# Weight conversion in a fused attention and two-expert kernel: background work placed by running sums of engine time, fetches on GpSimd's queue, all first-product weights through scratch

## The chip, the cores and the metric

The kernel runs on one core of a Trainium2 chip. TensorE (PE) multiplies, VectorE (DVE) and ScalarE (ACT) compute on tiles, GpSimd (POOL) and SyncE (SP) issue DMA transfers here. The metric is the time of one execution on the device in microseconds (us); less is better.

## The reference

What is computed, cut to its core (4 batches, 12 heads, 448 positions, head size 64; DM = 768, DFF = 2048; 1792 tokens):

```
scores = np.matmul(q, k.transpose(0, 1, 3, 2)) / np.sqrt(64) - np.log(448)
x = np.matmul(1.0 / (1.0 + np.exp(-scores)), v)      # to (1792, 768)
h = x @ moe_w_in                                     # (768, 2048)
x = (h - np.tanh(h)) @ moe_w_out                     # (2048, 768)
h = x @ moe2_w_in
out = (np.maximum(h, 0) + alpha * np.minimum(h, 0)) @ moe2_w_out
```

The activations are float32, and the four weight matrices are float64.

## The kernel before, in words

**Numbers.** Every product runs in float16 with two halves per operand: a value is scaled, its high half is its rounding to float16, and its low half is what is left (x*s - high). Three matmuls per tile pair (high-high, high-low, low-high) are added up in PSUM. A "split" writes both halves of a tile: ACT the high one, DVE the low one.

**Stages.** TensorE goes through 5088 matmul instructions in this order. Attention: 12 groups `g` of two head pairs, each with scores (L353, sigmoid on ACT in L355) in seven parts `u`, and values (L371, L377; float32) that add into one PSUM tile `ps3`, which DVE copies out (L384) and searches for its maximum (L300). The first product (`product(0, ...)`, L398): 16 column blocks `f` by 2 token halves `sb`, 36 matmuls each, with a chain of ACT and DVE operations after each (L655 to L664) that ends in a COPY_PREDICATED (L663). The second product (`product(1, ...)`, L398): 6 column blocks `e` by two halves, 96 matmuls each; its operands are the results `g` of the first, split by `split_job` (L292, L293) once their scale is known (`scale_jobs`, L247 to L262). Then the second expert by Strassen's scheme: seven products by four quarters `q` by two halves, 18 matmuls each, into (L744) and out (L826). Its operands are split in L425 and L426; PSUM results are copied in L751 and added in L756.

**Weights.** A float64 weight comes in as pairs of int32 words, in 64 "units" of six 128x128 blocks (768 KB). `load_unit` fetches one into one of two buffers `stage0`, `stage1` (L104, on SP's queue). Three DVE operations (L110, L112, L114) turn the pairs into float32 words; a split follows (L128, L129 for the first two matrices, L154, L155 for the quarters of the second expert's matrices, where sums and differences of four units are made first, L165 to L183). The 16 units of the first matrix stay in slots; all others are written to scratch in DRAM by GpSimd's queue (L134, L156) and read again by SP's when needed (L219 for the second matrix, L558 for the quarters). There are 53 general slots of 128x896 float32; a slot that is released is given to the next that asks.

**Order.** The conversion is a generator (`conv`), and `bg(us)` takes steps from it, or from the waiting `jobs`, until their estimated lengths reach the number given. These numbers are written at each place of the program: `1.2*len(us)` after each part of attention, 2.2 or 4.0 in the first product, 17.0 in the second, 0.4 to 3.0 in the second expert. `ahead` bounds how many units attention may convert. The order in which an engine runs its instructions is then fixed by a scheduler when the program is built, and each engine and each queue goes through its own list in that order.

Of the kernel before, what the change touches and what calls it, by code (L numbers as in the profile page):

```python
# [35 lines left out]
NG = NP // 2  # L36
# [20 lines left out]

@with_exitstack
def body(ctx: ExitStack, tc, qkd, vd, w1, w2, w3, w4, al, out):
    nc = tc.nc  # L60
    V, A, PE = nc.vector, nc.scalar, nc.tensor
# [7 lines left out]
    scratch.update({(1, u): dr_pool.tile([128, 2 * UN * 128], F16, name=f"scr1_{u}") for u in range(NU)})  # L69
# [30 lines left out]
    def load_unit():  # L100
        i = loaded[0]
        if i < 4 * NU:
            src = wd[i // NU][i % NU].bitcast(I32)
            nc.sync.dma_start(out=stage[i % NSTAGE].rearrange("p a b -> p (a b)"), in_=src)  # L104
            loaded[0] += 1

    def words(i, w):
# [3 lines left out]
        yield 0.57  # L111
        V.scalar_tensor_tensor(w, hi, -0x40000000, w, ALU.bitwise_and, ALU.bitwise_or)  # L112
        yield 0.96
        V.scalar_tensor_tensor(w, lo, 29, w, ALU.logical_shift_right, ALU.bitwise_or)  # L114
        load_unit()
        yield 0.96

    def pair_of(s):
        return s.bitcast(F16)[:, 0:2 * UN * 128].rearrange("p (a c) -> p a c", a=2)

    def conv():
        for i in range(2 * NU):
            w = w32[i % 2]
            yield from words(i, w)
            wf = w.bitcast(F32)
            s = alloc()
            v = pair_of(s)
            A.activation(v[:, 0], wf, AF.Copy, scale=SW)  # L128
            V.scalar_tensor_tensor(v[:, 1], wf, SW, v[:, 0], ALU.mult, ALU.subtract)  # L129
            nconv[0] += 1  # L130
            if i < NU:
                wslot[0, i] = s
            else:
                nc.gpsimd.dma_start(out=scratch[1, i - NU], in_=s.bitcast(F16)[:, 0:2 * UN * 128])  # L134
                release(s)
            yield 0.96
        for m in (2, 3):
            for q in range(NQ):
                yield from quarter(m, q)


    def quarter(m, q):
# [8 lines left out]
        def put(pr, s, scale=SW2):  # L151
            t = alloc()
            v = pair_of(t)
            A.activation(v[:, 0], fl(s), AF.Copy, scale=scale)  # L154
            V.scalar_tensor_tensor(v[:, 1], fl(s), scale, v[:, 0], ALU.mult, ALU.subtract)  # L155
            nc.gpsimd.dma_start(out=scratch[m, pr, q], in_=t.bitcast(F16)[:, 0:2 * UN * 128])  # L156
            release(t)
            return 0.96
# [7 lines left out]
        yield 0.87  # L166
        yield put(5, r)
        yield put(4, a22, -SW2)
# [4 lines left out]
        yield 0.87  # L173
        yield put(6, r)
        V.tensor_tensor(fl(a21), fl(a11), fl(a21), ALU.subtract)
        yield 0.87
        yield put(7, a21)
        release(a21)
        yield put(1, a11)
# [4 lines left out]
        yield 0.87  # L184
        yield put(3, r)
        release(r)
        yield put(2, a12)
# [8 lines left out]
    ahead = [4 * NU]  # L196

    def conv_step(force=False):
        if nconv[0] >= 4 * NU or (not force and (len(free) <= reserve[0] or nconv[0] >= ahead[0])):
            return None  # L200
        return next(conv_gen, 0.0)

    def weight(m, n):
        while (m, n // UN) not in wslot:
            if m:
                load_second(n // UN + 1)
            else:
                conv_step(True)
# [3 lines left out]
    second = [0]  # L212

    def load_second(upto):
        while second[0] < min(upto, NU):
            while nconv[0] <= NU + second[0]:
                conv_step(True)
            t = alloc()
            nc.sync.dma_start(out=t.bitcast(F16)[:, 0:2 * UN * 128], in_=scratch[1, second[0]])  # L219
            wslot[1, second[0]] = t  # L220
            second[0] += 1
# [65 lines left out]
    def split_job(d, key, g):  # L287
        def f():
# [3 lines left out]
            A.activation(v[:, 0], src, AF.Copy, scale=s_of(g))  # L292
            V.scalar_tensor_tensor(v[:, 1], src, s_of(g), v[:, 0], ALU.mult, ALU.subtract)  # L293
# [29 lines left out]
    def split_pair(i, parts=1):  # L323
# [4 lines left out]
        for j in range(parts):  # L328
            sl = slice(j * n, (j + 1) * n)
            if parts > 1 and j:  # L330
                V.tensor_scalar(v[:, 0, sl], t[:, sl], SQK, None, ALU.mult)  # L331
            else:
                A.activation(v[:, 0, sl], t[:, sl], AF.Copy, scale=SQK)  # L333
        for j in range(parts):
            sl = slice(j * n, (j + 1) * n)
            V.scalar_tensor_tensor(v[:, 1, sl], t[:, sl], SQK, v[:, 0, sl], ALU.mult, ALU.subtract)  # L336
# [25 lines left out]
    def values(g, u):  # L362
# [18 lines left out]
        if u == 6:  # L381
            b, j = divmod(g, H // 4)
# [39 lines left out]
    def split_to(src, n, g):  # L422
        t = alloc()
        v = hl(t)
        A.activation(v[:, 0, 0:n], src[:, 0:n], AF.Copy, scale=s_of(g))  # L425
        V.scalar_tensor_tensor(v[:, 1, 0:n], src[:, 0:n], s_of(g), v[:, 0, 0:n], ALU.mult, ALU.subtract)  # L426
# [109 lines left out]
    def bgo(us, most):  # L536
        while us > 0 and ojobs and len(opo) < most and len(free) > 6:
            us -= ojobs.pop(0)()
# [37 lines left out]
    if True:  # L576
# [15 lines left out]
        last = None  # L592
        for g in range(NG):
# [3 lines left out]
            if g == NG // 2:  # L597
                jobs.extend(scale_jobs(0, KD))
                jobs.extend(unit_jobs(0))
                jobs.extend(split_job(x, (j, b), 0) for b in range(2) for j in range(KD // 2))  # L600
            ahead[0] = 4 * g // 5
            for n, us in enumerate(groups):
# [9 lines left out]
                if last is not None:  # L612
                    for u in last[1]:
                        values(last[0], u)
                        if u == 6 and last[0] + 3 <= NG - 1:
# [290 lines left out]
```

## Time and profile before

| what | us |
|---|---|
| median of 3 timed runs (1024.02 to 1029.5) | 1025.11 |
| the profiled execution, its own time | 1028.73 |
| span of its trace | 1027.0 |
| TensorE busy | 963.3 |
| VectorE busy | 720.9 |
| ScalarE busy | 577.6 |

The profiled execution lies 3.6 us above the median. A trace gives each instruction's start and length on its engine, and for idle time what ended it. The granted clock of TensorE is 1.00 at 2.4 GHz and 0.50 at 1.2 GHz; a window's mean lies between.

### The profile page before, as it was taken

The numbers are of one execution on the slowest core, as the hardware profiler recorded it, in microseconds if no ns is written. First come the engines' busy times: TensorE is split into PE (matmuls) and PEld (weight loads), VectorE is DVE, ScalarE is ACT, GpSimd is POOL, SyncE is SP. The second block draws the span as 40 slices with busy tenths as digits, with TensorE's granted clock in tenths as the row PEclk, the third lists the DMA queues.
The fourth block names the chain that finished last, engine by engine and source line by source line (L and its number), as shares of the span: only waits on it lengthen the run. The fifth ranks groups of instructions, "written<-read, shape, count | busy, mean of one in ns | idle before, by whom it ended". The sixth has DMA issues, their size and how long they took to land. (4 is left out here: it accounts for less than half of the span.)

```text
span 1027.0 us, 13246 instructions
## 1 busy us (share of the span) xinstructions
PE 963.3 (94%) x5280; PEld 468.2 (46%) x5280; DVE 720.9 (70%) x869; ACT 577.6 (56%) x708; POOL 43.9 (4%) x87
## 2 busy tenths in 40 slices
PE   6888999999999998999499986999999999999998
PEld 2222335555555554555254542455555544555554
DVE  5845749988898897899898788844444789664200
ACT  7777867988999898433333226533333636434200
POOL 0000000000000000111111110000000000000000
PEclk9998999999999998999799998899999999999999
DMA  9833311222242401487888763432522336346301
GB/s 357 294 133 115 117 50 44 81 74 93 77 170 77 138 21 43 165 307 284 305 302 302 267 224 119 152 115 87 161 85 77 93 94 210 108 162 211 120 28 54
DMA packets 42398, 151.87 MB, mean 148 GB/s; under 512 B 5344, under 2 KB 8672, under 8 KB 42336
## 3 DMA queue, kind: packets, MB, share of 16 engines
q1 hardware_dynamic: 36576, 122.71, 36.0%
q0 software_dynamic: 5760, 28.32, 7.3%
q8 instruction: 41, 0.67, 0.3%
q14 instruction: 21, 0.17, 0.0%
HBM read 117.19 MB, written 33.82 MB: 147 GB/s over the span
## 5 line engine op out<-in xcount | busy, mean ns | idle before, releaser
L398 PE MATMUL ps<-slot,slot 128*128 128x448 f16 x2304 | 440.6, 355 | 18.5 <-DMA slot<-scr 14.6
L398 PEld LDWEIGHTS <-slot 128*128 128x128 f16 x2304 | 226.2, 98 | 233.2 <-DMA slot<-scr 13.3
L744 PE MATMUL ps<-slot,slot 128*128 128x448 f16 x1008 | 196.2, 358 | 15.8 <-ACT slot L751 9.8
L826 PE MATMUL ps<-slot,slot 128*128 128x448 f16 x1008 | 193.9, 354 | 4.6 <-ACT slot L425 2.6
L744 PEld LDWEIGHTS <-slot 128*128 128x128 f16 x1008 | 99.9, 99 | 111.9 <-issue 22.5
L826 PEld LDWEIGHTS <-slot 128*128 128x128 f16 x1008 | 99.0, 98 | 99.3 <-issue 8.9
L425 ACT ACTIVATE slot<-slot,sc 128x896 f16<-128x896 f32 (+1 forms) x78 | 77.1, 1026 | 76.4 <-PE ps L826 38.2
L154 ACT ACTIVATE slot<-slot 128x768 f16<-128x768 f32 x56 | 46.7, 842 | 114.9 <-DVE slot L114 56.1
L426 DVE SCALAR_TENSOR_TENSOR slot<-slot,sc,slot 128x896 f16<-128x896 f32 (+1 forms) x78 | 85.8, 1134 | 35.5 <-ACT slot L425 35.3
L355 ACT ACTIVATE slot<-ps,cst 128x896 f32<-128x896 f32 x84 | 79.8, 1004 | 21.4 <-PE ps L353 21.4
L371 PE MATMUL ps<-slot,slot 128*64 128x448 f32 x288 | 66.3, 584 | 11.5 <-DVE slot L384 10.9
L353 PE MATMUL ps<-slot 64*128 64x448 f16 (+1 forms) x576 | 59.8, 368 | 8.9 <-DVE slot L331 4.9
L756 DVE TENSOR_TENSOR slot<-ps,slot 128x896 f32<-128x896 f32 x24 | 26.2, 1090 | 50.9 <-ACT slot L751 46.1
L155 DVE SCALAR_TENSOR_TENSOR slot<-slot,slot 128x768 f16<-128x768 f32 x56 | 51.9, 951 | 1.1 <-ACT slot L154 1.0
L661 DVE SCALAR_TENSOR_TENSOR slot<-ps,sc,slot 128x896 f32<-128x896 f32 x32 | 36.7, 1148 | 22.2 <-ACT slot L659 22.2
L293 DVE SCALAR_TENSOR_TENSOR slot<-slot,sc,slot 128x896 f16<-128x896 f32 x44 | 48.1, 1145 | 4.5 <-ACT slot L292 4.5
L751 ACT ACTIVATE slot<-ps 128x896 f32<-128x896 f32 x24 | 21.8, 908 | 48.5 <-PE ps L744 48.5
L353 PEld LDWEIGHTS <-slot 64*128 64x128 f16 (+1 forms) x576 | 22.4, 100 | 56.7 <-issue 38.4
L292 ACT ACTIVATE slot<-slot,sc 128x896 f16<-128x896 f32 x44 | 42.7, 1029 | 7.3 <-DVE sc L261 7.3
L336 DVE SCALAR_TENSOR_TENSOR slot<-slot,slot 128x896 f16<-128x896 f32 (+1 forms) x25 | 26.3, 1051 | 25.6 <-ACT slot L333 25.5
L762 ACT ACTIVATE slot<-slot 128x896 f32<-128x896 f32 x24 | 22.7, 947 | 37.4 <-DVE slot L761 37.4
L664 ACT ACTIVATE slot<-slot,sc 128x896 f32<-128x896 f32 x32 | 33.3, 1039 | 13.2 <-DVE slot L663 13.2
(78 smaller groups left out, 841.4 us busy)
## 6 DMA issues: line engine op xcount, KB each, us to landing
stage<-w SPq DMA_DIRECT2D x64, 768.0 KB, 4.6
slot<-scr SPq DMA_DIRECT2D x128, 384.0 KB, 3.2
scr<-slot POOLq DMA_DIRECT2D x72, 384.0 KB, 3.2
slot<-qk SPq DMA_DIRECT2D x23, 448.0 KB, 7.3
slot<-v SPq DMA_DIRECT2D x12, 448.0 KB, 6.3
out_t<-slot SPq DMA_DIRECT2D x24, 224.0 KB, 2.0
slot<-qk SPq DMA_DIRECT2D x2, 224.0 KB, 2.6
alpha<-al SPq DMA_DIRECT2D x1, 8.0 KB, 7.3
```

The lines of the kernel that those rows point to most:

```text
L154: A.activation(v[:, 0], fl(s), AF.Copy, scale=scale)
L155: V.scalar_tensor_tensor(v[:, 1], fl(s), scale, v[:, 0], ALU.mult, ALU.subtract)
L292: A.activation(v[:, 0], src, AF.Copy, scale=s_of(g))
L293: V.scalar_tensor_tensor(v[:, 1], src, s_of(g), v[:, 0], ALU.mult, ALU.subtract)
L353: PE.matmul(p[rows, h, 0:S], v[r, jk, S + c * 128:S + c * 128 + m], v[r, jq, 0:S], start=(n == 0), stop=(n == 2), skip_group_check=True)
L355: A.activation(two(a), p[:, :, 0:S], AF.Sigmoid, scale=1.0 / (8.0 * SQK * SQK), bias=cst[:, 0:1])
L371: PE.matmul(p[64 * h:64 * h + 64, i, 0:S], v[:, o:o + 64], a[:, h], start=(c == 0), stop=False, skip_group_check=True)
L398: PE.matmul(p[:, b, 0:S], w[:, i], act(k, sb, b)[:, j], start=(k == 0 and (i, j) == (0, 0)), stop=(k == nk - 1 and (i, j) == (1, 0)))
L425: A.activation(v[:, 0, 0:n], src[:, 0:n], AF.Copy, scale=s_of(g))
L426: V.scalar_tensor_tensor(v[:, 1, 0:n], src[:, 0:n], s_of(g), v[:, 0, 0:n], ALU.mult, ALU.subtract)
L744: PE.matmul(p[:, i, 0:S], w[:, x1, 3 * i + c], a[:, x2], start=fresh and c == 0 and n == 0, stop=c == 2 and n == 2, skip_group_check=True)
L826: PE.matmul(bank(banks[e]), w[:, x1, 2 * e + c], a[:, x2, c * S:(c + 1) * S], start=pr in (1, 2, 5) and q == 0 and c == 0 and n == 0, stop ...
```

## The change

There are five parts.

1. A class `Engine` wraps the three compute engines and adds an estimated length of each instruction to a running sum (`V.t`, `A.t`, `PE.t`) as the program is written out. An operation that touches PSUM starts no earlier than the sum of TensorE. `bg(lead, most)` now emits background work while the sum of DVE (or of ACT, less `most`) is behind that of TensorE; the hand-written numbers and `ahead` go. In the trace of the changed kernel all such operations have the line of the wrapper's call (L81).
2. A split puts its high half on DVE if DVE's sum is behind ACT's (`halves_of`), else on ACT as before. In the built program 70 high halves have moved: 46 of 128x896 and 24 of 128x768.
3. The stage fetches go from SP's queue to GpSimd's (L133).
4. The 16 units of the first matrix go through scratch too (L161, L251): 16 more writes (88 in all) and 16 more reads by SP. Two or three units are loaded ahead of their use instead of five at the start of the second product.
5. In attention the values lag two parts behind their scores instead of one, and background work is also placed ahead of the copy of a group.

```diff
+class Engine:
...
+            if op == "matmul":
+                part = args[0].shape[0] * args[0].shape[1] / 16384
+                self.t += part * n * (1.68e-3 if args[0].dtype == F32 else 0.421e-3) + (0.01 if part < 1 else 0.0)
+            else:
+                if any(a.space == bass.MemoryType.PSUM for a in used):
+                    self.t = max(self.t, self.pe.t)
+                    rate = 1.04e-3
+                else:
+                    rate = 0.52e-3 if op == "tensor_scalar" else 1.04e-3
+                self.t += n * (0.83e-3 if op == "activation" else rate) + (0.26 if op == "activation" else 0.16)
+            return f(out, *args, **kw)
...
-            nc.sync.dma_start(out=stage[i % NSTAGE].rearrange("p a b -> p (a b)"), in_=src)
+            nc.gpsimd.dma_start(out=stage[i % NSTAGE].rearrange("p a b -> p (a b)"), in_=src)
...
+    def halves_of(hi, lo, src, scale):
+        if V.t + 0.4 < A.t:
+            V.tensor_scalar(hi, src, scale, None, ALU.mult)
+        else:
+            A.activation(hi, src, AF.Copy, scale=scale)
+        V.scalar_tensor_tensor(lo, src, scale, hi, ALU.mult, ALU.subtract)
...
+    def load_units(upto):
+        while taken[0] < min(upto, 2 * NU):
+            i = taken[0]
+            while nconv[0] <= i:
+                conv_step(True)
+            t = alloc()
+            nc.sync.dma_start(out=t.bitcast(F16)[:, 0:2 * UN * 128], in_=scratch[i])
...
-    def bg(us):
-        while us > 0:
+    def bg(lead=0.0, most=1.0):
+        while max(V.t, A.t - most) < PE.t + lead:
             if jobs:
-                us -= jobs.pop(0)() or 0.0
-                continue
-            c = conv_step()
-            if c is None:
+                jobs.pop(0)()
+            elif not conv_step():
+                V.t = max(V.t, PE.t + lead - 2.0)
                 return
-            us -= c
...
         if u == 6:
+            if g:
+                bg(-1.0, 4.0)
...
-            ahead[0] = 4 * NU
-            if f >= KF - 2:
-                load_second(3 * (f - KF + 2) + 2 * sb)
-            bg(4.0 if (jobs and f > 8) else 2.2)
+            load_units(f + 3 if sb == 0 else 0)
+            bg()
...
-            load_second((min(e + 1, KD) * KF + UN - 1) // UN + 1)
+            load_units(NU + (min(e + 1, KD) * KF + UN - 1) // UN + 1)
             reserve[0] = 3
-            ahead[0] = 4 * NU
...
-            bg(17.0)
+            bg()
```

How the built order moves, in three places. In the rows a name's last number is the program's own; `scr1_2` before and `scr_18` after are the same unit of the second weight, `scr1_9` and `scr_25` another.

SP's queue before, ahead of the second product:

```order
L219 DMA slot14_149<-scr1_1_120 128x1536
L219 DMA slot15_150<-scr1_0_119 128x1536
L104 DMA stage1_189<-w2 128x1536
L219 DMA slot52_187<-scr1_2_121 128x1536
L104 DMA stage0_188<-w2 128x1536
L219 DMA slot2_137<-scr1_3_122 128x1536
```

The unit `scr1_2` is reloaded here among the units loaded ahead of the second product, into `slot52`.

SP's queue before, at the seventh of that product's twelve parts:

```order
L219 DMA slot20_155<-scr1_10_129 128x1536
L104 DMA stage1_189<-w3 128x1536
L219 DMA slot13_148<-scr1_11_130 128x1536
L104 DMA stage0_188<-w3 128x1536
L219 DMA slot2_137<-scr1_9_128 128x1536
L104 DMA stage1_189<-w3 128x1536
L104 DMA stage0_188<-w4 128x1536
```

Each reload (L219) stands behind a stage fetch (L104).

SP's queue in the changed kernel, over the same two places:

```order
L251 DMA slot11_162<-scr_16_135 128x1536
L251 DMA slot36_187<-scr_17_136 128x1536
L251 DMA slot46_197<-scr_22_141 128x1536
L251 DMA slot37_188<-scr_20_139 128x1536
L251 DMA slot33_184<-scr_21_140 128x1536
L251 DMA slot50_201<-scr_18_137 128x1536
L251 DMA slot0_151<-scr_19_138 128x1536
L251 DMA slot2_153<-scr_23_142 128x1536
L251 DMA slot15_166<-scr_24_143 128x1536
L251 DMA slot6_157<-scr_27_146 128x1536
L251 DMA slot17_168<-scr_26_145 128x1536
L251 DMA slot2_153<-scr_25_144 128x1536
```

The stage fetches are gone from between the reloads; `scr_18` goes to `slot50` and comes behind `scr_22`, `scr_20` and `scr_21`.

DVE in the changed kernel, the end of the first product's last chain (`ps3`), with splits of the second product's operands between:

```order
L81 SCALAR_TENSOR_TENSOR slot48_199<-slot28_179,sc_212,slot48_199 128x896
L81 COPY_PREDICATED slot20_171<-slot40_191,ps2_215 128x896
L81 SCALAR_TENSOR_TENSOR slot0_151<-slot0_151,ps3_216 128x896
L81 SCALAR_TENSOR_TENSOR slot19_170<-slot32_183,sc_212,slot19_170 128x896
L81 SCALAR_TENSOR_TENSOR slot23_174<-slot10_161,sc_212,slot23_174 128x896
L81 SCALAR_TENSOR_TENSOR slot30_181<-ps3_216,sc_212,slot0_151 128x896
L81 SCALAR_TENSOR_TENSOR ps3_216<-ps3_216,sc_212,slot16_167 128x2x448
L81 SCALAR_TENSOR_TENSOR slot40_191<-slot29_180,sc_212,slot40_191 128x896
L81 COPY_PREDICATED slot30_181<-slot50_201,ps3_216 128x896
```

The last row reads `slot50`, so the reload of `scr_18` above stands behind it; before, that unit went to `slot52`, which was free earlier.

DVE at the start of the program before, from the second pair's split on:

```order
L336 SCALAR_TENSOR_TENSOR slot9_144<-slot1_136,slot9_144 128x896
L336 SCALAR_TENSOR_TENSOR slot14_149<-slot3_138,slot14_149 128x896
L590 TENSOR_SCALAR nalpha_193<-alpha_192 128x16
L336 SCALAR_TENSOR_TENSOR slot18_153<-slot4_139,slot18_153 128x896
L336 SCALAR_TENSOR_TENSOR slot27_162<-slot10_145,slot27_162 128x896
L336 SCALAR_TENSOR_TENSOR slot31_166<-slot11_146,slot31_166 128x896
L110 TENSOR_SCALAR w32_0_190<-stage0_188 128x768
L112 SCALAR_TENSOR_TENSOR w32_0_190<-stage0_188,w32_0_190 128x768
L114 SCALAR_TENSOR_TENSOR w32_0_190<-stage0_188,w32_0_190 128x768
```

The conversion of the first unit (`w32_0`) begins behind these splits.

The same in the changed kernel, from the first row:

```order
L81 SCALAR_TENSOR_TENSOR slot6_157<-slot0_151,slot6_157 128x448 x2
L81 TENSOR_SCALAR w32_0_206<-stage0_204 128x768
L81 TENSOR_SCALAR slot9_160<-slot1_152 128x896
L81 SCALAR_TENSOR_TENSOR w32_0_206<-stage0_204,w32_0_206 128x768
L81 SCALAR_TENSOR_TENSOR slot9_160<-slot1_152,slot9_160 128x896
L81 SCALAR_TENSOR_TENSOR w32_0_206<-stage0_204,w32_0_206 128x768
L81 TENSOR_SCALAR slot14_165<-slot3_154 128x896
L81 TENSOR_SCALAR slot37_188<-w32_0_206 128x768
L81 SCALAR_TENSOR_TENSOR slot14_165<-slot3_154,slot14_165 128x896
```

It has moved to between the first splits of the scores' operands, and high halves (TENSOR_SCALAR into a slot) have come to DVE.

## Rows read from the trace of the kernel before

**Rows 1.** Busy time of the engines over the whole span, from the page: us (share of the span) and instructions.

```profile
PE 963.3 (94%) x5280; PEld 468.2 (46%) x5280; DVE 720.9 (70%) x869; ACT 577.6 (56%) x708; POOL 43.9 (4%) x87
```

**Rows 2.** The waits of TensorE, summed up by what ended them: us in total, times, longest.

```profile
PE ps L398 <- DMA slot<-scr: 14.6, 2, 12.9
PE ps L371 <- DVE slot L384: 10.9, 6, 3.5
PE ps L744 <- ACT slot L751: 9.8, 2, 8.1
PE ps L744 <- ACT slot L425: 5.3, 1, 5.3
```

**Rows 3.** Windows of 25 us: length, then busy us (and instructions) of PE, PEld, DVE, ACT and POOL, then the mean granted clock, the DMA share and GB/s.

```profile
375.00:400.00 25.00, 21.05 (x99) 10.08 (x98) 20.96 (x23) 22.11 (x28) 0.35 (x1) 0.86 0.10 31
450.00:475.00 25.00, 25.00 (x134) 12.91 (x132) 22.59 (x29) 9.54 (x13) 3.96 (x8) 1.00 0.82 285
475.00:500.00 25.00, 18.89 (x100) 9.59 (x98) 21.43 (x26) 9.13 (x13) 4.86 (x9) 0.93 0.85 299
500.00:525.00 25.00, 18.20 (x88) 9.08 (x89) 22.36 (x27) 9.09 (x12) 3.77 (x7) 0.80 0.85 312
600.00:625.00 25.00, 19.02 (x90) 9.07 (x88) 23.53 (x38) 12.38 (x15) 3.34 (x6) 0.86 0.77 261
625.00:650.00 25.00, 15.22 (x66) 7.09 (x65) 23.52 (x38) 16.19 (x21) 0.65 (x1) 0.80 0.35 111
```

**Rows 4.** The timeline of TensorE around 500 us: start, length, what; in brackets the idle time before and what ended it.

```profile
492.22 1.68 PE L398 MATMUL ps<-slot,slot 128*128 128x448 f16 x8
506.80 5.37 PE L398 MATMUL ps<-slot,slot 128*128 128x448 f16 x19 [12.90 <-DMA slot<-scr]
```

**Rows 5.** The timeline of SP's queue around 495 us: start, the time in which the entries were issued, what.

```profile
493.56 0.33 SPq L219 DMA_DIRECT2D slot<-scr  x1
497.61 0.33 SPq L104 DMA_DIRECT2D stage<-w  x1
498.03 0.57 SPq L219 DMA_DIRECT2D slot<-scr  x1
```

**Rows 6.** The DMA issues by kind, from the page: queue, count, KB each, median us to landing.

```profile
stage<-w SPq DMA_DIRECT2D x64, 768.0 KB, 4.6
slot<-scr SPq DMA_DIRECT2D x128, 384.0 KB, 3.2
scr<-slot POOLq DMA_DIRECT2D x72, 384.0 KB, 3.2
```

**Rows 7.** The spread of the landing times in the views of two lines: first the stage fetches (L104), then the scratch writes of the quarters (L156).

```profile
DMA to landing us min/median/max: 3.9/4.6/10.1
...
DMA to landing us min/median/max: 2.6/4.0/7.5
```

**Rows 8.** Groups of instructions by line and form: busy us, mean ns of one, idle time before them.

```profile
L155 DVE SCALAR_TENSOR_TENSOR slot<-slot,slot 128x768 f16<-128x768 f32 x56 | 51.9, 951 | 1.1 <-ACT slot L154 1.0
...
L154 ACT ACTIVATE slot<-slot 128x768 f16<-128x768 f32 x56 | 46.7, 842 | 114.9 <-DVE slot L114 56.1 <-issue 26.5 <-DMA scr<-slot 13.1
L292 ACT ACTIVATE slot<-slot,sc 128x896 f16<-128x896 f32 x44 | 42.7, 1029 | 7.3 <-DVE sc L261 7.3
...
L112 DVE SCALAR_TENSOR_TENSOR slot<-stage,slot 128x768 int32<-128x768 int32 x32 | 30.4, 954 | 0.5
...
L110 DVE TENSOR_SCALAR slot<-stage 128x768 int32<-128x768 int32 x32 | 17.6, 556 | 24.1 <-DMA stage<-w 13.6 <-issue 7.0 <-DMA scr<-slot 3.5
```

**Rows 9.** The waits of DVE for a stage fetch: us in total, times, longest.

```profile
DVE slot L110 <- DMA stage<-w: 13.6, 10, 4.1
```

**Rows 10.** The timeline of DVE in the first 30 us, two operations: a high half of 448 elements, and the copy of the first group.

```profile
4.48 0.38 DVE L331 TENSOR_SCALAR slot<-slot 128x448 f16<-128x448 f32 x1
...
24.10 1.08 DVE L384 COPY slot<-ps 128x896 f32<-128x896 f32 x1
```

**Rows 11.** The timeline of TensorE at the start of the second product.

```profile
388.31 0.90 PE L398 MATMUL ps<-slot,slot 128*128 128x448 f16 x2 [3.18 <-ACT slot L292]
389.98 7.25 PE L398 MATMUL ps<-slot,slot 128*128 128x448 f16 x27 [0.77 <-DVE slot L293]
```

**Rows 12.** The timeline of DVE from the first half's scale on.

```profile
361.87 0.21 DVE L261 TENSOR_SCALAR sc<-sc 128x1 f32<-128x1 f32 x1
...
363.21 4.33 DVE L293 SCALAR_TENSOR_TENSOR slot<-slot,sc,slot 128x896 f16<-128x896 f32 x4
...
396.52 1.19 DVE L663 COPY_PREDICATED slot<-slot,ps 128x896 f32<-128x896 int32 x1
```

**Rows 13.** The timeline of DVE ahead of the second expert.

```profile
594.50 1.03 DVE L110 TENSOR_SCALAR slot<-stage 128x768 int32<-128x768 int32 x2 [7.01 <-issue]
...
616.59 0.15 DVE L261 TENSOR_SCALAR sc<-sc 128x1 f32<-128x1 f32 x1
```

**Rows 14.** The timeline of TensorE at the start of the second expert.

```profile
617.87 0.53 PE L744 MATMUL ps<-slot,slot 128*128 128x448 f16 x1 [5.33 <-ACT slot L425]
...
644.38 7.85 PE L744 MATMUL ps<-slot,slot 128*128 128x448 f16 x26 [8.07 <-ACT slot L751]
```

More of the change, by code (lines that the diff above doesn't have):

```diff
@@ L55, with __init__, __getattr__, call @@
 LAG = 4
+class Engine:
+    def __init__(self, raw, pe=None):
+        self.raw, self.pe, self.t = raw, pe, 0.0
+    def __getattr__(self, op):
+        f = getattr(self.raw, op)
+        def call(out, *args, **kw):
+            used = [a for a in (out, *args) if hasattr(a, "space")]
+            n = int(np.prod((args[0] if op == "tensor_reduce" else out).shape[1:]))
+            if op == "matmul":
[9 more added lines that the diff above has]
+            return f(out, *args, **kw)
+        return call
 @with_exitstack
@@ L68, in body @@
                for m in (2, 3) for pr in range(1, 8) for q in range(NQ)}
-    scratch.update({(1, u): dr_pool.tile([128, 2 * UN * 128], F16, name=f"scr1_{u}") for u in range(NU)})
+    scratch.update({u: dr_pool.tile([128, 2 * UN * 128], F16, name=f"scr_{u}") for u in range(2 * NU)})
     slots = [sb_pool.tile([128, T2], F32, name=f"slot{i}") for i in range(NSLOT)]
@@ L124, in conv @@
             yield from words(i, w)
[L125 to L129, printed above, removed]
-            nconv[0] += 1
[L131 to L136, printed above, removed]
+            to_scratch(i, w.bitcast(F32), SW)
+            nconv[0] += 1
+            yield
         for m in (2, 3):
@@ L151, in put @@
         def put(pr, s, scale=SW2):
[L152 to L158, printed above, removed]
+            to_scratch((m, pr, q), fl(s), scale)
         f = []
@@ L165, in quarter @@
         V.tensor_tensor(fl(r), fl(a21), fl(a22), ALU.add)
-        yield 0.87
-        yield put(5, r)
-        yield put(4, a22, -SW2)
+        yield
+        put(5, r)
+        yield
+        put(4, a22, -SW2)
+        yield
         release(a22)
@@ L329, in split_pair @@
             sl = slice(j * n, (j + 1) * n)
[L330 to L336, printed above, removed]
+            halves_of(v[:, 0, sl], v[:, 1, sl], t[:, sl], SQK)
         release(t)
@@ L534, in out_jobs, with bgo @@
         return seq + [put(3, 1, 1, q, True) for q in range(NQ)]
-    def bgo(us, most):
-        while us > 0 and ojobs and len(opo) < most and len(free) > 6:
-            us -= ojobs.pop(0)()
+    def bgo(most=9):
+        while ojobs and len(opo) < most and len(free) > 6 and max(V.t, A.t) < PE.t + 3.0:
+            ojobs.pop(0)()
     stream = []
@@ L591, in body, with values_of @@
         groups = ((0, 1), (2, 3), (4, 5, 6))
-        last = None
+        def values_of(g, us):
+            for u in us:
+                values(g, u)
+            if u == 6 and g == NG // 2 - 1:
+                jobs.extend(scale_jobs(0, KD))
+                jobs.extend(unit_jobs(0))
+                jobs.extend(split_job(x, (j, b), 0) for b in range(2) for j in range(KD // 2))
+        todo = []
         for g in range(NG):
@@ L611, in body @@
                     split_pair(2 * g + 1 + n)
[L612 to L615, printed above, removed]
-                            pass
+                todo.append((g, us))
+                if len(todo) > 2:
+                    values_of(*todo.pop(0))
                 if n == 0 and g and g + 1 < NG:
                     load_values(g + 1)
-                last = g, us
-                bg(1.2 * len(us))
-        for u in last[1]:
-            values(last[0], u)
+                reserve[0] = 8
+                if g:
+                    bg(-1.0, 4.0)
+        load_units(3)
+        for each in todo:
+            values_of(*each)
         flush()
```

89 lines of the change are left out of this document (42 added, 47 removed).

## The prediction

> **What bounds the kernel now.** I read the busy shares first: TensorE works in 963.3 of 1027.0 us, VectorE (DVE) in 720.9, ScalarE (ACT) in 577.6 [rows 1]. The end is set by TensorE, and only what makes TensorE stand still or run at the low clock can be won. Next come the waits of TensorE [rows 2]: the largest is 14.6 us in the first two products for a weight tile that is reloaded from scratch, 12.9 of it in one wait; then 10.9 us in attention for the copy of a finished group (L384), and 9.8 and 5.3 us at the seam into the second expert's input product. The windows of 25 us say what each place costs, clock included [rows 3]: an undisturbed window has 134 matmuls, so one matmul is 25/134 = 0.187 us. From 475 to 525 there are 100 + 88, so 80 are missing: 14.9 us. From 600 to 650 there are 90 + 66, 112 missing: 20.9 us. From 375 to 400 there are 99, 35 missing: 6.5 us. These three places, 42 us together, are what the change can win or lose; call them B, S (the seam) and A.
>
> **B, the reload (L219).** TensorE stops after 493.9 us for 12.90 us [rows 4]. SP's queue shows why [rows 5]: the reload that ends the wait is issued at 498.03, behind a stage fetch at 497.61 for which SP stood since 493.56, because the fetch overwrites a buffer that DVE still reads (SP's order is fixed, and this fetch stands ahead). The changed order has no stage fetch on SP at all, so the reload goes out when its slot is free. In the new order the tile in question (scr_25) gets its slot when 2495 matmuls are issued and is needed by matmul 2532: 37 x 0.187 = 6.9 us, against a reload's 3.2 us median [rows 6]. I take all of it: **-15 (-15 to -8)**, the lower gain if the reload lands late. The other 1.7 of the 14.6 us goes the same way: **-2**.
>
> **The price of that, GpSimd's queue.** 64 fetches of 768 KB move there, beside 72 writes that become 88. The trace has no load on this queue. Its nearest rows: writes of 384 KB there land in 3.2 us median, SP's reads of the same size in 3.2, SP's stage fetches in 4.6 [rows 6]; spread, the fetches 3.9 to 10.1, the writes of one line 2.6 to 7.5 [rows 7]. A fetch has a double buffer ahead of it. Its room, in the tightest place of the Strassen quarters, is one unit's three word operations (0.56 + 2 x 0.95), one sum and two low halves (3 x 0.95), together 5.3 us [rows 8]; for the first two matrices one unit and one low half, 4.4 us. I take a landing of about 4.6 as on SP, since the two queues agree on 384 KB, and cost it at **0** while DVE has its 13.6 us of such waits already, the longest 4.1 [rows 9]. At the slow end it is the rival below. What is queued behind a fetch that waits for its buffer is only the next scratch write, and no engine needs that soon, except the second-product tiles, which the sum above has 6.9 us for.
> The word operation L110 and the low halves fill DVE in these stretches (22.6 us busy of 25 between 450 and 475, rows 3), and writes from GpSimd's queue landed beside them in 3.2 us. The Trainium skill (SBUF — State Buffer, section "SBUF: two separate sides") says the opposite is to be feared: a DVE operation in a two-port mode keeps GpSimd from writing descriptors, and 620 ns became some 3100 there. By that rule the fetches would land some 2.5 us later, an estimate from its figures, and the sum would be that of the rival; the rows of the writes don't bear it out so far.
>
> **ACT to DVE.** 70 high halves move: 46 of 128x896 and 24 of 128x768. On ACT one of 768 takes 0.84 us; on DVE a tensor_scalar of 448 takes 0.38 [rows 8, 10], so I put one of 896 at about 0.6. ACT loses 46 x 1.03 + 24 x 0.84 = 68 us, DVE gains about 40 us: its share rises, and DVE is what TensorE waits for at the places below. Where it lands decides, so each stage is costed from the new order, times durations of the old trace.
>
> **Attention: 0 (-5 to +8).** DVE's work up to the copies of the first four groups grows from 46.5 to 64.0 us by the order (unit 0 and 1 are now converted at the very start, ahead of the later splits); in time, about 64 x 0.95 (independent operations start closer than they last) + 4 us before the first + 3 us of waits = 67 us for the fourth copy, where the trace has about 62.5. Against that, values now follow two steps behind their scores instead of one, so each copy (1.08 us, rows 10) has 2.5 us more before TensorE feels it, and the 10.9 us of waits for it [rows 2] are what that covers. 5 late at the start, 5 won after: nothing. The first two fetches now leave at once and share the transfers with the first tiles, and GpSimd's library load (L279) moves from the start into its queue of fetches; both are in the upper end. In product 0 the new order has the same DVE work as the old (185.7 against 186.3 us): 0.
>
> **A, the start of the second product: +7 (0 to +10).** Before, five tiles of the second weight are loaded ahead, and TensorE stops at about 385 for 3.18 and 0.77 us for high and low half of an operand [rows 11]. Now only two are loaded ahead. The third (scr_18) goes to slot50, which the last COPY_PREDICATED of product 0 still reads; it is needed at matmul 1992, at 385. From the scale (361.87 in the trace) 30 instructions of DVE stand up to it, 26 long ones at 1.07 from start to start (4.33 for four) and 4 short ones at 0.55: 30.0 us, so 392 [rows 12]; the old trace has the same operation at 396.5, held by ACT, which now has four activations less. Plus 3.2 to 4 us of reload: TensorE goes on at 396, 11.4 us late, instead of 4. That is 7 more; both clock dips are alike. If the load is preponed by a quicker chain it is nothing.
>
> **S, the seam: -11 (-20 to -3).** Before, all 64 units are converted by the time the second input product begins, and DVE is behind: the scale of the first half is done at 616.59, and DVE had idled 7.01 us before 594.50 [rows 13]; TensorE waits 5.33 and 8.07 us, and the low clock follows [rows 14]. With the running sums five units (about 24 us of DVE work) stay behind and are converted inside that product, where DVE is little used. DVE work per product of 18.2 us falls from 20.3 to 15.6 to 19.8 in the last four. If DVE is in time, 1 or 2 of 20.9 us remain; if it is 10 us late, as its rate of 22.6 in 25 allows, about 11 remain plus half of the rest. I take the middle. The five units cost something behind: in the first four quarters DVE gets 12.6 to 15.6 us per 13.6 of TensorE: **+4 (0 to +9)**. The output product: 0.
>
> **Sum**: 0 + 7 - 15 - 2 - 11 + 4 = -17. The profiled execution took 1028.73 us, so 1011.7. It lies 3.6 us above the median of 1025.11, and on that basis the forecast is 1008.
>
> **Rivals.**
> Late fetches (slower): if a fetch on GpSimd's queue takes 7.5 us, the slowest of its writes [rows 7], DVE stands 2.2 us per unit in the six products where it is full: 20 units x 2.2 = 44 us, of which 14 are caught up in the lighter products that follow; it decides from a landing of 5.3 us on. The seam then grows by 30 instead of shrinking by 11, the rest as above: 1028.7 + 7 - 17 + 30 = 1049, about 1045 by the median. For it: a fetch moves twice the bytes of a write, and two fetches and two writes can stand in that queue at once. Against: the writes' median of 3.2. Chance 0.14.
> The sums don't see waits, and DVE is as late as before at the seam: S is 0, and the five units come on top: 7 - 17 + 4 = -6, by the median 1019. For it: the model counts 0.16 us an instruction and no wait for a landing. Chance 0.18.
> All goes well: A as before, S almost gone, the output product a little better: -17 - 19 - 3 = -39, 986 by the median. For it: the chain of A runs ahead when ACT is relieved. Chance 0.17.
> Attention is DVE-bound from the start and gives 8 us away: 1016. Chance 0.10.
>
> **How the numbers follow.** The forecast has 0.41. Faster by over 0.5% (about what a measurement of this kernel can tell from no change) is under 1020: forecast, the good case, the attention case and a little over half of the blind sums, some mishaps taken off, 0.71. Same: 0.12. Slower, over 1030: the late fetches and the unknown, 0.17. The range goes from 989, just above the good case, to 1034, where the worst tenth begins.
>
> **What would show it.** Right: the wait of 12.9 us for a reload gone, the window 475 to 525 with some 260 matmuls; a wait of about 11 us for a reload at the start of the second product; at the seam fewer than 8 us of waits for the splits and for the copy that L751 makes now; stage landings of about 4.6 us on GpSimd's queue. Wrong: DVE's waits for the stage far above 13.6 us, ACT's halves waiting for DVE, or a wait of TensorE for L384 beyond the first groups of attention. A second product that starts without a stop would make A wrong, and a wait of over 5 us for a split at the seam would make S wrong.

## The result, and the profile after

The changed kernel takes 1039.39 us in the median (1037.2 to 1041.09, 4 runs) against 1024.71 (1024.02 to 1029.5, 4 runs): 1.0132 times as long, interval 1.0094 to 1.0170. The forecast was 1008, with 989 to 1034 as the range; the change is slower, and outside the range. The profiled execution took 1040.48 us, 11.75 more than that of before. By the medians the change costs 14.7 us; the traces explain the two profiled executions, and the 3 us between stay unplaced.

Busy times, from the page; compare [rows 1]. DVE has 37 us more work and ACT 56.5 less, where some 40 and 68 were costed.

```profile
PE 963.9 (93%) x5280; PEld 468.4 (45%) x5280; DVE 758.0 (73%) x938; ACT 521.1 (50%) x639; POOL 87.9 (8%) x167
```

The waits of TensorE, summed up (us in total, times, longest); compare [rows 2]. All wrapped operations have line L81.

```profile
PE ps L81 <- DVE slot L81: 29.5, 13, 5.4
PE ps L81 <- ACT slot L81: 24.1, 8, 7.6
PE ps L81 <- DMA slot<-scr: 16.3, 3, 10.4
```

The windows, as in [rows 3]; the count behind PE is what to read, 134 being a full window:

```profile
375.00:400.00 25.00, 17.19 (x87) 8.30 (x86) 24.35 (x32) 17.82 (x23) 0.35 (x1) 1.00 0.13 42
...
475.00:500.00 25.00, 23.20 (x123) 11.80 (x121) 18.75 (x23) 7.09 (x10) 6.07 (x12) 1.00 0.80 265
500.00:525.00 25.00, 22.11 (x110) 11.14 (x111) 21.36 (x27) 8.15 (x11) 6.25 (x13) 0.93 0.77 260
575.00:600.00 25.00, 14.59 (x62) 6.65 (x61) 15.04 (x19) 8.18 (x12) 3.88 (x8) 0.73 0.56 187
600.00:625.00 25.00, 20.03 (x106) 10.27 (x105) 20.99 (x34) 5.95 (x8) 5.98 (x11) 1.00 0.86 301
625.00:650.00 25.00, 15.57 (x72) 7.39 (x72) 24.41 (x41) 16.56 (x20) 0.71 (x1) 0.84 0.52 168
650.00:675.00 25.00, 22.48 (x111) 11.22 (x111) 23.71 (x31) 13.69 (x20) 1.64 (x3) 0.88 0.47 147
```

Both traces run the same 5088 matmul instructions, so the start of one and the same matmul in either tells where the 11.7 us came from. (Matmuls are counted in the built order: the first product begins at 768, the second at 1920, the second expert at 3072. The seam is the end of the second product and the start of the second expert.)

| stretch | forecast | measured | how |
|---|---|---|---|
| attention | 0 | +2.1 | the first product starts at 155.6, before at 153.4 |
| A, start of the second product | +7 | +2.2 | 87 matmuls in the window, 99 before |
| B and the second reload | -17 | -10.2 | 233 between 475 and 525 against 188 (-8.4), and the second stop gone (-1.8) |
| last reload, near 581 | none | +13.4 | 62 in the window, 134 before |
| S, the seam | -11 | -0.5 | matmul 2976 to 3216: 66.1 us, before 66.6; undisturbed 45.4 |
| second expert, in | +4 | +2.9 | to matmul 3648 |
| second expert, out | 0 | +1.8 | to the end |

The sum is 11.7. The 13.4 us stood in no sum of the prediction: 10.4 are a stop, the other 3 the low clock behind it (granted 0.73 in the window). TensorE there:

```profile
592.03 8.13 PE L81 MATMUL ps<-slot,slot 128*128 128x448 f16 x27 [10.41 <-DMA slot<-scr]
```

SP issues the reload of the last unit (scr_31, into slot2) only here:

```profile
586.13 0.32 SPq L251 DMA_DIRECT2D slot<-scr  x1
```

and GpSimd the scratch write out of the same slot just before:

```profile
583.32 0.54 POOL L161 DMA_DIRECT2D scr<-slot  x1 [5.97 <-DVE slot L81]
```

In the built order this write stands ahead of matmul 2809, which TensorE reached at 556.7. Background work had got slot2 in between, DVE did it 27 us after its place, and the reload had to wait for the write to land. I call this distance (start of a DVE instruction, less the time at which TensorE reached the matmul beside which it stands) DVE's **debt**.

The DMA issues, as in [rows 6], with the first tiles' loads:

```profile
slot<-scr SPq DMA_DIRECT2D x144, 384.0 KB, 3.4
stage<-w POOLq DMA_DIRECT2D x64, 768.0 KB, 5.2
scr<-slot POOLq DMA_DIRECT2D x88, 384.0 KB, 4.6
slot<-qk SPq DMA_DIRECT2D x23, 448.0 KB, 10.7
```

Fetches land in 5.2 us instead of 4.6, the tiles of attention in 10.7 instead of 7.3 (page of before). DVE's waits for a stage, in all; compare the 13.6 of [rows 9]:

```profile
DVE slot L81 <- DMA stage<-w: 34.2, 13, 5.3
DVE w L81 <- DMA stage<-w: 12.0, 6, 4.8
```

### The profile page after: what moved, and what is told of

It is laid out like the page before. It is cut to its first block, busy times and chain, and to the rows that moved or that the text cites. A ratio compares the mean times of both kernels' runs of the same rounds, so it can differ in the third digit from the quotient of the medians.

```text
span 1038.7 us, 13345 instructions
## 1 busy us (share of the span) xinstructions
PE 963.9 (93%) x5280; PEld 468.4 (45%) x5280; DVE 758.0 (73%) x938; ACT 521.1 (50%) x639; POOL 87.9 (8%) x167
## 4 chain that ended last, share of the span: by engine, by line
PE 36%; DVE 27%; issue 19%; DMA 9%; ACT 7%; POOL 2%; SPq 0%; POOLq 0%; DVEq 0%; ACTq 0%
PE ps L81 36%; DVE slot L81 20%; ACT slot L81 6%; DMA stage<-w 6%; DVE w L81 3%; DVE ps L81 3%; DMA scr<-slot 1%; DMA slot<-qk 1%; POOL scr L161 1%; POOL stage L133 1%; DVE sc L81 0%; DMA slot<-scr 0%; POOL sc L279 0%; DMA out_t<-slot 0%; DVE mx L81 0%
## 5 line engine op out<-in xcount | busy, mean ns | idle before, releaser
L81 PE MATMUL ps<-slot,slot 128*128 128x448 f16 (+2 forms) x4704 | 907.2, 373 | 61.3 <-DVE slot L81 24.9
L81 PEld LDWEIGHTS <-slot 128*128 128x128 f16 (+2 forms) x4896 | 447.6, 99 | 511.6 <-issue 95.2
L81 ACT ACTIVATE slot<-slot,sc 128x896 f16<-128x896 f32 (+1 forms) x163 | 163.3, 1031 | 116.0 <-PE ps L81 46.4
L81 ACT ACTIVATE slot<-slot 128x896 f32<-128x896 f32 (+2 forms) x116 | 103.9, 898 | 183.4 <-DVE slot L81 151.6
L81 DVE SCALAR_TENSOR_TENSOR slot<-slot,sc,slot 128x896 f16<-128x896 f32 (+1 forms) x122 | 134.3, 1140 | 23.4 <-ACT slot L81 22.8
L81 DVE SCALAR_TENSOR_TENSOR slot<-slot,slot 128x768 f16<-128x768 f32 (+3 forms) x105 | 104.5, 1007 | 17.1 <-ACT slot L81 16.0
L81 ACT ACTIVATE slot<-ps,cst 128x896 f32<-128x896 f32 x84 | 79.8, 1005 | 65.7 <-PE ps L81 65.3
L81 DVE SCALAR_TENSOR_TENSOR slot<-ps,sc,slot 128x896 f32<-128x896 f32 (+1 forms) x50 | 48.6, 982 | 81.4 <-ACT slot L81 55.7
L81 DVE TENSOR_TENSOR slot<-slot,slot 128x768 f32<-128x768 f32 (+2 forms) x82 | 75.0, 933 | 4.4 <-PE ps L81 3.2
L81 ACT ACTIVATE slot<-ps,sc 128x896 f32<-128x896 f32 (+1 forms) x56 | 45.8, 835 | 62.4 <-PE ps L81 59.8
L161 POOL DMA_DIRECT2D scr<-slot x88 | 48.3, 549 | 319.6 <-DVE slot L81 267.1
L81 ACT ACTIVATE slot<-ps 128x896 f32<-128x896 f32 x52 | 46.4, 908 | 50.4 <-PE ps L81 50.3
L81 PE MATMUL ps<-slot 64*128 64x448 f16 (+1 forms) x576 | 61.0, 378 | 9.2 <-DVE slot L81 4.6
L81 ACT ACTIVATE slot<-slot,cst 128x896 f32<-128x896 f32 x64 | 66.4, 1038 | 1.4
L81 DVE SCALAR_TENSOR_TENSOR slot<-stage,slot 128x768 int32<-128x768 int32 x64 | 60.6, 955 | 1.2
L81 DVE SCALAR_TENSOR_TENSOR w<-stage,w 128x768 int32<-128x768 int32 x64 | 60.9, 956 | 0.8
L133 POOL DMA_DIRECT2D stage<-w x64 | 35.1, 549 | 226.1 <-DVE w L81 133.4
L81 DVE TENSOR_TENSOR slot<-ps,slot 128x896 f32<-128x896 f32 x24 | 26.1, 1089 | 32.0 <-ACT slot L81 28.7
L81 PEld LDWEIGHTS ps<-slot,slot 128*64 128x64 f32 (+1 forms) x384 | 20.9, 139 | 53.9 <-issue 37.5
L81 DVE TENSOR_SCALAR slot<-stage 128x768 int32<-128x768 int32 x32 | 17.8, 557 | 35.7 <-DMA stage<-w 34.2
L81 DVE COPY_PREDICATED slot<-slot,ps 128x896 f32<-128x896 int32 x32 | 38.2, 1193 | 0.5
L81 DVE SCALAR_TENSOR_TENSOR ps<-ps,sc,slot 128x896 f32<-128x896 f32 x32 | 36.9, 1154 | 0.0
## 6 DMA issues: line engine op xcount, KB each, us to landing
slot<-qk SPq DMA_DIRECT2D x23, 448.0 KB, 10.7
alpha<-al SPq DMA_DIRECT2D x1, 8.0 KB, 11.7
```

The lines of the kernel that those rows point to most:

```text
L81: return f(out, *args, **kw)
L133: nc.gpsimd.dma_start(out=stage[i % NSTAGE].rearrange("p a b -> p (a b)"), in_=src)
L161: nc.gpsimd.dma_start(out=scratch[key], in_=t.bitcast(F16)[:, 0:2 * UN * 128])
```

## The experiments

Theory 1: DVE's debt in the second product sets the loss. Theory 2: late fetches on GpSimd's queue. Theory 3: the turn of single reloads, by slot and place in the queue. Each group of four ran beside the kernel before; times of different groups are compared by their ratio to it. A ratio comes with its 95% interval. In e1 to e4 before took 1027.01 us, in e5 to e8 1027.74, in e9 to e12 1026.24.

**e1: the changed kernel, fetches on SP.**

```diff
-            nc.gpsimd.dma_start(out=stage[i % NSTAGE]...
+            nc.sync.dma_start(out=stage[i % NSTAGE]...
```

> The changed kernel with the stage fetches back on SP's queue, all else as changed. Theory 1 (VectorE, not a queue, sets the pace of the second product: its conversions fall some 30 us behind TensorE there in either kernel, and the debt is paid at whichever reload or seam comes first): the time stays within 8 us of the changed kernel, 1031 to 1043, with the debt paid at another place. Theory 2 (the fetches on GpSimd's queue come late and starve VectorE): the waits for the stage fall to some 15 us from 46, and the time to about 1015 to 1022. Theory 3 (only the slot of the last reload is at fault): the stop of 10.4 us stays, 1037 to 1041.

1027.01 us, ratio 0.9997 (0.9974 to 1.0019): the whole loss is gone, and the other four parts of the change show neither gain nor loss together. (Of these only part 2 was tried alone, in e5.) Fetches land in 4.5 us and the tiles of attention in 6.8, and attention is 2 us shorter:

```profile
stage<-w SPq DMA_DIRECT2D x64, 768.0 KB, 4.5
slot<-qk SPq DMA_DIRECT2D x23, 448.0 KB, 6.8
```

The queue is not all that moves: the scheduler also places some 50 of DVE's operations elsewhere. With the fetches on SP the first unit's conversion stands behind the first splits in both kernels (before, e1), with GpSimd's queue between them (after, e2). No run parts this order from the queue itself.

But the stop at B is back, and longer. Waits of TensorE between 400 and 680 us:

```profile
PE ps L81 <- DMA slot<-scr: 18.4, 1, 18.4
PE ps L81 <- ACT slot L81: 7.9, 2, 7.6
```

In this stop DVE works off its debt, 20.7 us at matmul 2496 and under 5 at 2592; the last reload then comes in time and the seam loses 10.2 us instead of 20.7. So the stops are linked: one pays for the next.

**e2: the kernel before, fetches on GpSimd's queue** (the same line, the other way).

> The kernel before with the stage fetches on GpSimd's queue and nothing else changed. Theory 1: the stop of 12.9 us at the reload shrinks, since nothing stands ahead of the reload on SP, and another stop of that size comes later in the second product or at the seam; 1020 to 1030. Theory 2: slower than before by most of the change's loss, 1033 to 1040. The forecast's own sum, with no debt of VectorE: 1008 to 1012.

1033.08 us, ratio 1.0060 (1.0038 to 1.0082). Waits of TensorE between 400 and 680 us:

```profile
PE ps L398 <- DMA slot<-scr: 19.5, 2, 9.9
PE ps L744 <- ACT slot L751: 8.0, 2, 6.3
```

The stop at B shrinks from 12.9 to 9.5 us and does not go: SP now stands until 498.7 for another reload ahead of it, whose slot DVE frees late (25.3 us of wait, for L155). A second stop of 9.9 us follows. Neither 1 nor 2 by itself. The 6 us are a balance: in the profiles B and the seam win 9.0 us, the second stop with its low clock takes back 10.5, and attention costs 2.3.

**e3, e4: no conversion beyond 52 units in the second product.** e3 is the changed kernel, e4 the kernel before.

```diff
-        if nconv[0] >= 4 * NU or (not force and len(free) <= reserve[0]):
+        if nconv[0] >= 4 * NU or (not force and (len(free) <= reserve[0] or nconv[0] >= ahead[0])):
...
             reserve[0] = 3
+            ahead[0] = 52
...
                 reserve[0] = 5
+                ahead[0] = 4 * NU
```

> The changed kernel, but in the second product no conversion starts once 52 of the 64 units are done; the other 12 (some 50 us of VectorE's work) follow in the second expert's input product. Nothing is left out. Theory 1: VectorE keeps up at the last reload and at the seam, so the stop of 10.4 us goes and the seam loses most of its 20 us: 1005 to 1014. Theory 2: the fetches stay as late as they are and starve VectorE in the second expert's input product instead: 1030 or more. Theory 3: only the one stop goes, 1024 to 1028.

> The kernel before with the same bound of 52 units in the second product, nothing left out. Theory 1: VectorE is less behind at the seam, which loses most of its 20 us, and the stop at the reload shrinks if it came from VectorE's debt: 998 to 1012. Theory 2 has no late fetches to remove here: 1020 to 1028.

e3: 1017.18 us, 0.9900 (0.9847 to 0.9953); e4: 1015.29 us, 0.9884 (0.9846 to 0.9922). In both the seam loses under 1 us instead of 21. In the rest of the second expert's input product, where the 12 units now lie, e3 loses 13.5 us (the changed kernel 2.9). In e4 the stop at B stays at 13.9. The stop at the last reload of e3 is gone: scr_31 has another slot there, and is issued at 551.5. The profiled execution of e3 is the fastest of its four, 1010.83 us. Waits of TensorE in it between 400 and 680 us:

```profile
PE ps L81 <- DVE slot L81: 4.7, 2, 3.0
PE ps L81 <- ACT slot L81: 2.0, 2, 1.8
PE ps L81 <- DMA slot<-scr: 0.8, 1, 0.8
```

**e8: e3 with the fetches on SP.**

> The changed kernel with the fetches on SP's queue and the bound of 52 units in the second product, nothing left out. If the queue's price and VectorE's debt are two separate things that add up, this is below both single edits: 998 to 1010. If the bound alone removes what late fetches cost, it equals the bound alone, 1010 to 1018.

1027.69 us, 1.0008 (0.9980 to 1.0036): not a sum of two gains. With SP's fetches the stop at B is there again, 18.6 us where e3 has 0.8 or less:

```profile
PE ps L81 <- DMA slot<-scr: 18.6, 1, 18.6
PE ps L81 <- DVE slot L81: 4.5, 2, 3.0
```

So the forecast's reading of B was right as a mechanism: behind stage fetches on SP a reload waits. The Trainium skill (DMA: Bandwidth & Descriptors, section "Issuing engines are not separate DMA queues") says that starting transfers on several engines saves only the time to start them, since all run on the same 16 engines. The longer landings of attention's tiles agree with the shared engines; the 18.6 us don't agree with "only", since what is saved here is standing behind another transfer's wait.

**e5: every high half on ACT.**

```diff
-        if V.t + 0.4 < A.t:
+        if False:
```

> The changed kernel with every high half on ScalarE again; the fetches stay on GpSimd's queue. If VectorE's short operations keep GpSimd from issuing its transfers (the rule that the forecast weighed), the landing of a stage fetch comes back from 5.2 to some 4.6 us and the time to about 1025. If the fetches are late because they share one queue and the transfers' bandwidth with 88 writes, the landing stays at 5.0 to 5.3 us. VectorE then has some 45 us less to do over the whole, but little of it in the second product, where ScalarE has time anyway: 1033 to 1040 if its debt there decides.

1044.43 us, 1.0173 (1.0153 to 1.0193), if anything slower than the change (the intervals overlap). In the profiles it loses 4.2 us more in attention, 5.4 more at A and 6.6 more in the second expert's input product, and wins 6.2 at B and 5.2 at the seam. So the moved halves gain at the start and behind the seam and cost at the seam. (The difference at B may be chance: e3, in the changed kernel's order up to there, loses only 1.0 us.) Fetches still land in 5.3 us:

```profile
stage<-w POOLq DMA_DIRECT2D x64, 768.0 KB, 5.3
```

The rule of the Trainium skill that the prediction weighed (SBUF — State Buffer, "SBUF: two separate sides"), by which DVE's two-port operations hold up GpSimd's transfers, isn't borne out for the moved halves: 70 of the short operations fewer, and the same landing. The 64 short operations of the unit conversion stay in every run, so nothing is shown for them.

**e6: one word operation of three left out.** The weights lose their sign and top exponent bits.

```diff
-        V.scalar_tensor_tensor(w, hi, -0x40000000, w, ALU.bitwise_and, ALU.bitwise_or)
```

> The changed kernel without one of the three word operations of a unit: the sign and top exponent bits of the weights are left out of the computation, and 64 x 0.95 us of VectorE's work with it, some 25 of it in the second product. The fetches, the writes and the reloads are all there. Theory 1 (VectorE's debt): the stop of 10.4 us goes and the seam shrinks, 1000 to 1015. Theory 2 (the fetches set the pace, whatever VectorE has to do): VectorE only waits longer for the stage, above 60 us in all, and the time stays above 1025.

1015.35 us, 0.9889 (0.9864 to 0.9913). The seam loses 0.4 us, although the fetches land in 6.0 us here, later than in any other run. One stop for a reload remains, at another unit (scr_28):

```profile
PE ps L81 <- DMA slot<-scr: 13.3, 1, 13.3
```

With less work for DVE the debt at the seam is gone (1.1 us); a reload's turn can still be late.

**e7, e9: reloads asked for one unit earlier.** In e9 also `reserve[0] = 2`, so that DVE has about as much to do as in the changed kernel.

```diff
-            load_units(NU + (min(e + 1, KD) * KF + UN - 1) // UN + 1)
+            load_units(NU + (min(e + 1, KD) * KF + UN - 1) // UN + 2)
-            reserve[0] = 3
+            reserve[0] = 2
```

> The changed kernel with each reload of the second product asked for one unit earlier, nothing left out. Theory 3 (the slot of the last reload decides): the stop of 10.4 us before the last unit goes and nothing takes its place, 1024 to 1030. Theory 1: the debt remains and is paid at the seam or at an earlier reload, whose slots now come from background work that is just as late: 1033 to 1042.

> Reloads one unit earlier as in e7, and the bound of free slots for background work in the second product lowered from 3 to 2, so that VectorE gets as much work there as in the changed kernel (176 us by the order between matmuls 2016 and 2976, against 180 in the changed kernel and 162 in e7). Nothing is left out. If the place of the reload in its queue and its slot decide (theory 3): the stop of 10.4 us stays away and only the seam is as dear as in the changed kernel, 1018 to 1027. If VectorE's debt decides (theory 1): it is paid at a reload or the seam in full, 1030 to 1042.

Of both, only e9 has the second edit. e7: 1013.35 us, 0.9870 (0.9840 to 0.9901); e9: 1026.40 us, 1.0003 (0.9986 to 1.0020). Neither stops for a reload after the start of the second product. Waits of TensorE in e7 between 400 and 680 us:

```profile
PE ps L81 <- ACT slot L81: 5.4, 1, 5.4
PE ps L81 <- DVE slot L81: 3.6, 2, 2.5
```

In e7 the earlier reloads hold slots, so less background work finds one (164.6 us of DVE's work between matmuls 2016 and 3024, in the changed kernel 180.2), and the debt at the seam is 6 us. In e9 (177.2 us of work) it is 24, and the seam is dearer than in any other run. TensorE in e9 there:

```profile
613.42 0.53 PE L81 MATMUL ps<-slot,slot 128*128 128x448 f16 x1 [13.55 <-ACT slot L81]
...
637.15 8.14 PE L81 MATMUL ps<-slot,slot 128*128 128x448 f16 x30 [6.21 <-ACT slot L81]
```

This parts theories 1 and 3: the turn of a reload makes the stops within the product, the debt that is left makes the seam.

**e10: e7 with the fetches on SP.**

> e7 with the stage fetches on SP's queue. If SP's order costs (a reload behind a stage fetch that waits for VectorE): a stop of some 13 to 19 us near 495 us comes back, 1024 to 1032. If early reloads are free of that, the queue's own price is left and the run is faster than e7 by what late fetches cost: 1003 to 1010.

1006.19 us, 0.9811 (0.9776 to 0.9846), the fastest median. No stop for a reload between 400 and 680 us:

```profile
PE ps L81 <- ACT slot L81: 4.1, 2, 3.9
PE ps L81 <- DVE slot L81: 3.3, 1, 3.3
```

Against e7 this is the queue's price once its benefit isn't needed: 0.6%, some 6 us, 2.4 of them in attention. The two intervals just overlap, so its size is uncertain by most of itself.

**e11: the kernel before with the same earlier reloads; e12: e7 with five units preloaded.**

```diff
-            load_second((min(e + 1, KD) * KF + UN - 1) // UN + 1)
+            load_second((min(e + 1, KD) * KF + UN - 1) // UN + 2)
```

```diff
             load_units(f + 3 if sb == 0 else 0)
+            if f >= KF - 2:
+                load_units(NU + 3 * (f - KF + 2) + 2 * sb)
```

> The kernel before with each reload of the second product asked for one unit earlier, nothing left out; the fetches stay on SP's queue. If a reload's late turn is what the stop of 12.9 us comes from: 1005 to 1016. If SP's stage fetches hold any reload up, early or not: 1020 to 1028.

> e7, and five units of the second weight asked for in the last two blocks of the first product as before the change. If the start of the second product stops for the reload into the last chain's slot: 1.5 to 5 us less than e7, 1008 to 1012. If it stops for the splits of its operands, which VectorE does at that time: the same as e7, 1012 to 1015.

e11: 1008.29 us, 0.9821 (0.9789 to 0.9853). One number in one line of the kernel before is worth as much as the whole of e10, within the intervals. The stop at B is gone with the fetches still on SP; one later reload still stops TensorE:

```profile
PE ps L398 <- DMA slot<-scr: 4.9, 1, 4.9
```

e12: 1011.31 us, 0.9858 (0.9815 to 0.9902), not clear of e7. A is 5 us shorter than in e7, and the seam 5.2 us dearer (debt 10.5 us instead of 6.2): the stop that was taken away came back.

As forecasts of times the theories did badly. e1, e3, e4, e5, e7 and e8 lie outside every range given for them, e2 at the lower end of theory 2's, e6 0.35 us above theory 1's; only e9 to e12 lie within one. What follows rests on which stops went and came, not on these ranges.

## Why the prediction was wrong, step by step

Two steps failed: the last reload, which stood in no sum and cost 13.4 us, and S, costed at -11, of which 0.5 came. In both, DVE's debt was put too low: at nothing for the reload, at between nothing and 10 us for S.

**S, a step that failed.** It took the middle between DVE in time and DVE 10 us late, 11 of 20.9 us off; -0.5 came. The running sums, by which it expected DVE to be nearly in time, count durations and no waits. By durations DVE does keep up: between matmuls 2016 and 3024 its work is 180.2 us, and TensorE needs 190.7 undisturbed. But DVE also stood for 49.7 us there, of which TensorE's own stops gave back 19.7; so it was 19.8 us behind at matmul 3024, before 18.4. Where DVE stood between 400 and 611 us:

```profile
DVE slot L81 <- DMA stage<-w: 31.9, 12, 5.3
DVE slot L81 <- ACT slot L81: 11.1, 6, 4.1
DVE w L81 <- DMA stage<-w: 4.1, 3, 2.1
```

The prediction's own sign came, a wait of over 5 us at the seam (7.6). These waits of TensorE are put to ACT, and ACT waits for DVE (612 to 653 us):

```profile
ACT slot L81 <- DVE sc L81: 15.8, 2, 8.7
ACT slot L81 <- DVE slot L81: 6.8, 2, 6.3
```

What the seam costs is DVE's debt, over all runs (loss: time from matmul 2976 to 3216, less 45.4 us):

| | e3 | e8 | e4 | e6 | e10 | e7 | e1 | e12 | e11 | e2 | e5 | before | after | e9 |
|---|---|---|---|---|---|---|---|---|---|---|---|---|---|---|
| debt at 3024, us | 1.0 | 1.0 | 1.1 | 1.1 | 4.5 | 6.2 | 9.0 | 10.5 | 11.1 | 13.7 | 15.1 | 18.4 | 19.8 | 24.3 |
| loss at the seam, us | 0.3 | 0.3 | 0.7 | 0.4 | 6.7 | 7.4 | 10.2 | 12.6 | 12.1 | 15.2 | 15.5 | 21.1 | 20.7 | 26.1 |

The rival of the sums that don't see waits had this right, and gave 0 for S.

**The last reload, a term that was missing.** What would be late next, once B no longer stops, was not asked. The stop at B had cleared DVE's debt in the kernel before (15.9 us ahead of it, 1.5 behind); with half of it gone the debt grew to 33 us at matmul 2928, and the last reload, into a slot that late background work still held, cost 13.4. It could be read in the built order: the write out of slot2 and the reload into it stand 15 matmuls apart, and the use only 116 on, 24.8 us of TensorE's time in all. The write came 26.6 us late, took 2.8 us to land and the reload 5.8: together 10.4 us too long, the length of the stop.

**B, a size.** -15 was taken and -8.4 came: the reload was issued at 493.1, near the 491 of its slot, but landed 9.7 us later, beside another reload and a stage fetch, instead of 3.2. The median was the wrong row: before, this reload went out at 498.03 and TensorE went on at 506.80, 8.8 us later [rows 4, 5]. The -8.4 is also one execution's: e3 has the same order up to there, its reload landed in 7.6 us, and 13.7 came. Where the reload was asked for earlier (e7, e9, e10, e11, e12), 14.7 came, all of it, on either queue.

**The queue's price.** It was costed at 0 with 4.6 us a landing. The landing is 5.2, the price some 6 us in e7 against e10, and DVE's waits for the stage are 46.2 us, the prediction's own sign of being wrong. The rival of late fetches had its point at 5.3 us and its loss at the seam; the fetches stayed below, and the loss fell at the last reload. In e6 they land in 6.0 us, and the seam loses 0.4: the landing alone doesn't decide. That e1 is 13 us faster than the change is this price and the stops that it leads to; they can't be added up, since a stop pays debt off.

**A** was +2.2 instead of +7: TensorE had its reload at 395.9, as forecast (396), but came 2.1 us later, and no low clock followed (1.00 in the window, 0.86 before). Of the five stops there, 7.7 us, only the last, 1.2, is for the reload; the others are for operands that DVE was late with, so the time came out better than the path. **Attention** lost 2.1; that the fetches share the transfers with the first tiles stood in the upper end only. With one order up to there, before, e4 and e11 start the first product at 153.4, 149.8 and 151.3, so a single pair can't show 2 us. Of the changed kernel's runs, e1, e8 and e10 (SP) start it at 152.4 to 153.6, and after, e3, e7, e9 and e12 (GpSimd) at 154.4 to 156.3. Whether the tiles' landings or DVE's order at the start make that difference is open. The second expert's +2.9 was near its +4; the +1.8 at the end was not tried.

Two of the prediction's side sums don't come out. The rival of late fetches leaves out the +4 that it says it keeps (1053, not 1049), and the -19 of the good case is not worked out: A as before gives -7, a seam almost gone some -9. Neither bears on the forecast.

## What to carry to other kernels

Where one engine's background work runs behind another's pace, a stop that is taken away comes back as the next one: follow the debt to the end of the stretch, and price the seam by it. A plan by durations alone doesn't see waits. A reload's real need is its slot's last user and whatever stands ahead in its queue. Asking for it one unit earlier was worth 1.8% here (e11), while the change without its queue showed no gain (e1).

## What the runs showed of the hardware

With fetches on GpSimd's queue the loads on SP's landed later: 9.4 to 11.4 us for attention's tiles (medians of eight runs; 10.7 in the changed kernel) against 6.7 to 7.3 (six runs; 7.3 in the kernel before), where the first two fetches go out from 1.3 us on, on SP from 6.8 to 7.0; no run has the one without the other. The fetches themselves landed in 4.8 to 6.0 us there (median of a run; 6.0 in e6) against 4.5 to 4.7 on SP. A fetch went out 0.30 us after the last reader of its buffer on GpSimd's queue, 0.03 us on SP (medians of after and e1). At A, stops of 3.4, 0.7, 1.5, 0.8 and 1.2 us with up to 12 matmuls between them left the clock at 1.00 in the changed kernel; before, stops of 3.2 and 0.8 us were followed by the low one (0.86 in the window).
